# Softmax attention with pooled keys, two expert layers: order of the opening on VectorE and ScalarE

## The chip, the cores and the metric

One Trainium2 chip, one NeuronCore of it. The metric is device microseconds of one execution of the whole program, lower is better. TensorE (PE) multiplies, VectorE (DVE), ScalarE (ACT) and GpSimd (POOL) do elementwise work, SyncE (SP) issues all DMAs.

## The reference

Three stages, each on the output of the one before. All inputs are float32 but the weights, which are float64 and are converted on the chip.

```python
# 1. attention, q/k/v (8, 8, 576, 64): keys and values are means over 8 neighbours
k_p = k.reshape(B, H, Sp, 8, D).mean(axis=3)          # Sp = 72
v_p = v.reshape(B, H, Sp, 8, D).mean(axis=3)
attn = softmax(q @ k_p.T / sqrt(64));  x = attn @ v_p  # x: (4608, 512) after regrouping
# 2. expert layer: w_in (512, 2048), w_out (2048, 512)
g = relu(x @ w_in) ** 2;  y = g @ w_out
# 3. soft mixture: phi (512, 32), w1 (8, 512, 1024), w2 (8, 1024, 512)
logits = y @ phi;  d = softmax over tokens;  c = softmax over slots
slot_out = relu((d.T @ y) @ w1[e]) @ w2[e];  out = c @ slot_out
```

## The kernel before, in words

The 4608 tokens are 36 tiles of 128. Per tile, attention is six steps (`att_qT`, `att_sc`, `att_exp`, `att_norm`, `att_aT`, `att_av`): TensorE turns q (line 188), multiplies it with the pooled keys `kb` (line 204); VectorE takes the maxima `mx` (line 211), ScalarE the exponentials `es`, eight of 72 columns (line 215); VectorE normalises (lines 236 to 238); TensorE turns the weights (line 269), ScalarE copies them to `aT` (line 270), TensorE multiplies with the pooled values `vp` (line 281). The result x goes to SBUF as a rounded high part `xh`, cast by ScalarE (line 288), and a low part `xl`, subtracted by VectorE (line 289).

The first layer is cut into units (t, j): tile t times chunk j of w_in, one of 4 chunks of 512 columns. A unit is 12 matmuls (line 400) over 4 rows kk of the chunk with x and w each in a high and a low part, into one of two PSUM banks `l`. Behind it ScalarE takes the relu `r` (line 412), and the square `g` is made either on VectorE, from the bank and `r` (line 419), or on ScalarE from `r` alone (line 421); the table on the line that sets `sq` chooses. The order of the units is written out in `units`: (0, 0), (0, 1), (1, 0), (3, 1), (3, 0), (1, 1), (2, 0), (0, 2), ..., and from tile 4 on two tiles at a time.

Ahead of its first unit a chunk is converted from float64, one row (0, kk), (1, kk), ... after the other (`conv_in`, `to_f32`): a first step on ScalarE (line 306), two mask steps (lines 307 and 310), a product (line 314), an add (line 317) and a last step (line 318) on VectorE, where table `AE` sends some adds to GpSimd ("P"). Then ScalarE casts the high part (line 349) and GpSimd subtracts the low part (line 350). GpSimd's reads and writes here are of SBUF only, as are those of lines 307 to 318.

The keys and values of the first batch are pooled at the start: keys by TensorE (line 138); values half by TensorE (`pool_v`, line 154, copied out by ScalarE in line 155) and half by VectorE (`pool_v_dve`, line 161). All loads are issued by SyncE in program order: k, q of tile 0, chunk 0, v, q of tile 1, chunk 1. Chunk 2 and 3 follow when their staging buffers `st` are free. In the opening the order of the steps of tiles 0 to 3 comes from `seq`, sorted by places, with the conversions of chunks 0 and 1 at the places in `CP`. The framework then orders the instructions of each engine by a timeline of its own, within data dependencies; `tc.high_priority` and `tc.issue_after` shift that order. Later steps hang at numbered slots of the units (`at`), and the conversions of chunks 2 and 3 follow a relu (`paced`).

Of the kernel before, what the change touches and what calls it, by code (L numbers as in the profile page):

```python
# [17 lines left out]
def kernel(  # L18
# [21 lines left out]
    P = 128  # L40
# [17 lines left out]
    AE = "VVPVVPVPPVVVVPVV"  # L58
    CP = ((5, 6, 6, 6), (19, 19, 22, 23))
# [124 lines left out]
    def att_qT(t):  # L184
# [46 lines left out]
    def att_norm(t):  # L231
# [26 lines left out]
    def att_aT(t):  # L258
# [7 lines left out]
        for half in range(2):  # L266
# [3 lines left out]
            nc.scalar.copy(  # L270
# [30 lines left out]
    def to_f32(src, dst=None, eng=None):  # L301
        hi, lo = src[:, :, 1], src[:, :, 0]
# [19 lines left out]
        return dst  # L322
# [67 lines left out]
    def l1_half(t, j, half):  # L390
# [8 lines left out]
        for i in range(half * n, (half + 1) * n):  # L399
            nc.tensor.matmul(hp_t[t, j], steps[i][0], steps[i][1], start=(i == 0), stop=(i == 2 * n - 1))  # L400
        if half == 1:
# [8 lines left out]
            sq = "VVVAVAVV"[2 * j + t % 2]  # L410
# [424 lines left out]
    kb_from(0, pk0)  # L835
# [189 lines left out]
```

## Time and profile before

| | us |
|---|---|
| median of 3 runs | 817.59 |
| lowest, highest | 813.96, 825.13 |
| profiled execution, its own time | 814.64 |
| its span in the profile | 812.9 |
| TensorE busy | 759.5 (93%) |
| VectorE busy | 518.0 (64%) |
| ScalarE busy | 394.2 (48%) |
| GpSimd busy | 161.8 (20%) |

The profiled execution's own time holds some 1.7 us around the span. Busy shares are means over the whole program; the opening and the rest are far apart, which the rows below show by stretch. PEclk is the granted clock of TensorE as a share of 2.4 GHz.

### The profile page before, as it was taken

How to read it: one execution, taken by the hardware profiler on the slowest of the kernel's cores; microseconds unless marked ns; L12 is line 12 of the kernel's file. 1: busy time of each engine (PE TensorE's matmuls, PEld its weight loads, DVE VectorE, ACT ScalarE, POOL GpSimd, SP SyncE). 2: the span in 40 equal slices, each digit the busy share in tenths (PEclk: the TensorE clock that was granted, in tenths of full speed). 3: DMA queues.
4: the chain of work that ended last, by engine and by line, in shares of the span. 5: the costliest groups of instructions: out<-in, count | busy, mean ns of one | idle time of the engine just before them, and what ended most of it. 6: DMA issues, size and time to landing. Idle time of an engine off the chain costs nothing. (4 is left out here: it accounts for less than half of the span.)

```text
span 812.9 us, 14793 instructions
## 1 busy us (share of the span) xinstructions
PE 759.5 (93%) x5352; PEld 525.5 (65%) x5352; DVE 518.0 (64%) x1033; ACT 394.2 (48%) x1143; POOL 161.8 (20%) x172
## 2 busy tenths in 40 slices
PE   6699999979999999998999999979999999998993
PEld 6477677757667776675666766746666766663552
DVE  5986865586626777685858687685676564424333
ACT  3664555335547473454546462762565643331232
POOL 2532512067513300035005402400000000000000
PEclk8689999999999999999999999989999999999996
DMA  9755734657635884887597797757438424969999
GB/s 278 248 173 193 221 129 148 228 165 250 206 120 158 228 234 130 260 224 178 175 290 227 193 273 203 193 187 213 131 124 278 144 91 158 352 250 321 372 360 313
DMA packets 180857, 175.12 MB, mean 215 GB/s; under 512 B 47152, under 2 KB 138288, under 8 KB 180784
## 3 DMA queue, kind: packets, MB, share of 16 engines
q1 hardware_dynamic: 180784, 174.17, 68.6%
q8 instruction: 43, 0.70, 0.4%
q14 instruction: 30, 0.25, 0.1%
HBM read 126.94 MB, written 47.19 MB: 214 GB/s over the span
## 5 line engine op out<-in xcount | busy, mean ns | idle before, releaser
L400 PE MATMUL l<-w,xh 128*128 128x512 f32 x1152 | 383.7, 412 | 7.1 <-DVE g L419 6.0
L400 PEld LDWEIGHTS l<-w,xh 128*128 128x128 f32 x1152 | 208.3, 190 | 79.6 <-issue 21.4
L400 PE MATMUL l<-w,xl 128*128 128x512 f32 x576 | 229.0, 398 | 0.0
L412 ACT ACTIVATE r<-l 128x512 f32<-128x512 f32 x144 | 86.5, 601 | 167.9 <-PE l L400 165.7
L400 PEld LDWEIGHTS l<-w,xl 128*128 128x128 f32 x576 | 108.8, 189 | 26.0 <-issue 1.0
L254 ACT COPY aT<-turned 32x256 f32<-32x256 f32 (+1 forms) x168 | 67.8, 403 | 22.2 <-DVE turned L263 20.0
L419 DVE TENSOR_TENSOR g<-l,r 128x512 f32<-128x512 f32 x75 | 51.1, 684 | 42.3 <-ACT r L412 35.9
L131 POOL TENSOR_TENSOR kv<-kv 72x512 f32<-72x512 f32 x40 | 52.8, 1323 | 96.3 <-DMA kv<-in_v_dram 65.8
L456 DVE STREAM_TRANSPOSE turned<-turned 128x1024 f32<-128x1024 f32 x39 | 47.8, 1231 | 6.3 <-DMA turned<-g_dram 6.3
L215 ACT ACTIVATE es<-att,mx 128x72 f32<-128x72 f32 x120 | 36.9, 335 | 21.0 <-DVE mx L211 20.9
L317 POOL TENSOR_TENSOR tmp<-tmp 128x512 f32<-128x512 f32 x21 | 28.6, 1362 | 80.4 <-DVE tmp L314 80.4
L215 ACT ACTIVATE es<-gT,mx 128x72 f32<-128x72 f32 x120 | 36.8, 327 | 10.9 <-DVE mx L211 10.7
L419 DVE TENSOR_TENSOR tmp<-l,r 128x512 f32<-128x512 f32 x33 | 22.6, 685 | 28.2 <-ACT r L412 16.7
L256 DVE COPY aT<-turned 32x256 f32<-32x256 f32 (+1 forms) x120 | 35.9, 299 | 4.6 <-PE gT L281 2.9
L350 POOL TENSOR_TENSOR w<-tmp,w 128x512 fp32r<-128x512 f32 x16 | 29.0, 1822 | 45.6 <-ACT w L349 41.3
L133 POOL TENSOR_TENSOR kp<-kv 72x128 f32<-72x128 f32 x20 | 10.1, 523 | 130.5 <-PE att L174 130.5
L456 DVE STREAM_TRANSPOSE tmp<-tmp 128x1024 f32<-128x1024 f32 x25 | 30.7, 1230 | 4.1 <-DMA tmp<-g_dram 4.1
L132 POOL TENSOR_TENSOR kv<-kv 72x256 f32<-72x256 f32 x40 | 31.3, 791 | 0.7
L552 PE MATMUL misc<-g,d 128*32 128x512 f32 x134 | 25.8, 631 | 6.0 <-DVE d L542 5.9
L238 DVE TENSOR_TENSOR es<-es,rs 128x576 f32<-128x576 f32 x36 | 30.5, 846 | 1.0
L307 DVE TENSOR_SCALAR tmp<-tmp 128x512 uint32<-128x512 uint32 x32 | 17.6, 549 | 18.8 <-ACT tmp L306 18.8
L204 PE MATMUL gT<-kb,qT 128*128 128x144 f32 (+1 forms) x176 | 27.3, 306 | 0.0
(188 smaller groups left out, 1138.4 us busy)
## 6 DMA issues: line engine op xcount, KB each, us to landing
g_dram<-g SPq DMA_DIRECT2D x95, 256.0 KB
turned<-g_dram SPq DMA_DIRECT2D x156, 128.0 KB
w<-in_moe_w_dram SPq DMA_DIRECT2D x32, 512.0 KB
tmp<-g_dram SPq DMA_DIRECT2D x100, 128.0 KB
w<-in_moe_w_dram SPq DMA_DIRECT2D x6, 2048.0 KB
g_back<-g_dram SPq DMA_DIRECT2D x10, 1024.0 KB
kv<-in_k_dram SPq DMA_DIRECT2D x32, 288.0 KB
kv<-in_v_dram SPq DMA_DIRECT2D x32, 288.0 KB
```

The source lines that it names most:

```text
L131: eng.tensor_tensor(out=x[:, :, 0:4], in0=x[:, :, 0:4], in1=x[:, :, 4:8], op=ALU.add)
L132: eng.tensor_tensor(out=x[:, :, 0:2], in0=x[:, :, 0:2], in1=x[:, :, 2:4], op=ALU.add)
L215: nc.scalar.activation(out=es[:, e], in_=sv[:, h], func=AF.Exp, bias=mx[:, e:e + 1], accum_out=rsum[:, t % 8, e, 0:1],)
L238: nc.vector.tensor_tensor(out=es, in0=es, in1=rs.unsqueeze(2).to_broadcast([P, H, SP]), op=ALU.mult)
L254: nc.scalar.copy(out=dst, in_=src)
L256: eng[e].tensor_copy(dst, src)
L317: (eng or nc.gpsimd).tensor_tensor(out=mag, in0=mag, in1=low, op=ALU.add)
L350: nc.gpsimd.tensor_tensor(out=w[:, 1, kk], in0=c, in1=w[:, 0, kk].bitcast(F32), op=ALU.subtract)
L400: nc.tensor.matmul(hp_t[t, j], steps[i][0], steps[i][1], start=(i == 0), stop=(i == 2 * n - 1))
L412: nc.scalar.activation(out=r, in_=hp, func=AF.Relu, scale=1.0 / (R * R if sq == "V" else R))
L419: mark["sq"] = nc.vector.tensor_tensor(out=dst, in0=pre, in1=src, op=ALU.mult)
L456: nc.vector.transpose(out=gc.rearrange("p (n i) -> p n i", i=32), in_=gc.rearrange("p (n f) -> p n f", f=32))
```

## The change

It does five things, all in the first 170 us. The conversion is cut into four parts that can be placed singly (`f32_steps`, `conv_steps`). A new function `opening` writes the order out: tile 0's keys, scores, exponentials and normalisation get high priority, the pooling of v and the parts of chunk 0's conversion are placed behind marks of tile 0's attention, unit (0, 0) comes ahead of tile 1's scores, and chunk 1's conversion stands around tile 3's attention in the text. Row 2 of chunk 0 has its add on VectorE, not on GpSimd (`AE`). Rows 2 and 3 of chunk 0 are loaded behind v. All squares of tiles 0 to 5 are on ScalarE, where before 6 of 24 were.

```diff
-    AE = "VVPVVPVPPVVVVPVV"
+    AE = "VVVVVPVPPVVVVPVV"
...
     def to_f32(src, dst=None, eng=None):
+        steps = f32_steps(src, dst, eng)
+        for _ in range(3):
+            dst = next(steps)
+        return dst
+
+    def f32_steps(src, dst=None, eng=None):
...
         nc.scalar.activation(out=val, in_=hi.bitcast(F32), func=AF.Copy, scale=2.0 ** -112)
+        yield
...
+        yield
         (eng or nc.gpsimd).tensor_tensor(out=mag, in0=mag, in1=low, op=ALU.add)
...
-        return dst
+        yield dst
...
+    def conv_steps(j, kk):
...
+        steps = f32_steps(st_t["in", j][:, kk], eng=eng[AE[4 * j + kk]])
+        for _ in range(3):
+            c = next(steps)
+            yield
         nc.scalar.copy(out=w[:, 0, kk], in_=c)
         nc.gpsimd.tensor_tensor(out=w[:, 1, kk], in0=c, in1=w[:, 0, kk].bitcast(F32), op=ALU.subtract)
+        yield
...
-            sq = "VVVAVAVV"[2 * j + t % 2]
+            sq = "A" if t < 6 else "VVVAVAVV"[2 * j + t % 2]
...
-    load_w("in", 0)
+    load_w("in", 0, 0, 2)
     for i in range(NPAIR):
         load_kv(v, raw_v, 0, i)
+    load_w("in", 0, 2, 4)
...
-    kb_from(0, pk0)
...
-    seq = [(p, 1, lambda kk=kk, j=j: conv_in(j, kk)) for j in range(PC) for kk, p in enumerate(CP[j])]
-    seq += [(1, 0, v0)]
-    seq += [(i, 2, lambda i=i: steps[i % 6](i // 6)) for i in range(24)]
...
+    def opening():
+        conv = {(j, kk): conv_steps(j, kk) for j in range(PC) for kk in range(KD)}
+
+        def go(j, kk, n=4):
+            for _ in range(n):
+                next(conv[j, kk])
...
+        early(kb_from, 0, pk0)
+        go(0, 0, 2)
+        early(att_qT, 0)
+        go(0, 0, 1)
+        behind([("qT", 0), "kbA"], go, 0, 0, 1)
+        early(att_sc, 0)
+        go(0, 1, 1)
+        behind(["kbV"], go, 0, 1, 2)
+        behind([("es", 0)], go, 0, 1, 1)
+        early(att_norm, 0)
+        for i in range(0, NPAIR, 2):
+            behind([("sc", 0), ("es", 0)], pool_v, 0, i, kvp)
+            behind([("mx", 0) if i == 0 else ("norm", 0)], pool_v_dve, 0, i + 1, kvp)
+        go(0, 2, 1)
+        behind([("mx", 0)], go, 0, 2, 2)
+        behind([("es", 0)], go, 0, 2, 1)
+        early(att_aT, 0)
+        early(att_av, 0)
+        go(0, 3, 3)
+        behind([("aT", 0)], go, 0, 3, 1)
+        for half in range(2):
+            l1_half(0, 0, half)
+        att_qT(1)
+        behind([("aT", 0)], att_sc, 1)
+        att_norm(1)
+        behind([("l1", 0, 0)], att_aT, 1)
+        att_av(1)
+        for t in (2, 3):
+            att_qT(t)
+            for kk in range(2):
+                if t == 3:
+                    go(1, kk)
+            att_sc(t)
+            att_exp(t)
+            att_norm(t)
+            att_aT(t)
+            for kk in range(2, 4):
+                if t == 3:
+                    go(1, kk)
+            att_av(t)
+
+    opening()
```

The line numbers of the changed kernel differ by 1 to 15 in the lines named here; its orders below have its own numbers. VectorE in the program before, from the copy of tile 0's keys to its first maxima (`kb_119` are the keys, `vp` pooled values, `mx` maxima, `tmp` steps of the conversion):

```order
L167 COPY kb_119<-att 64x4x72
L318 SCALAR_TENSOR_TENSOR tmp<-tmp 128x512
L161 TENSOR_REDUCE vp<-kv_150 72x128
L314 SCALAR_TENSOR_TENSOR tmp<-st,tmp 128x512
L307 TENSOR_SCALAR tmp<-tmp 128x512
L310 TENSOR_SCALAR tmp<-tmp 128x512
L161 TENSOR_REDUCE vp<-kv_150 72x128
L211 TENSOR_REDUCE mx<-gT 128x4 x2
L314 SCALAR_TENSOR_TENSOR tmp<-st,tmp 128x512
```

VectorE in the changed program, the same stretch:

```order
L166 COPY kb_119<-att 64x4x72
L313 TENSOR_SCALAR tmp<-tmp 128x512
L316 TENSOR_SCALAR tmp<-tmp 128x512
L320 SCALAR_TENSOR_TENSOR tmp<-st,tmp 128x512
L324 TENSOR_TENSOR tmp<-tmp 128x512
L210 TENSOR_REDUCE mx<-gT 128x4
L325 SCALAR_TENSOR_TENSOR tmp<-tmp 128x512
L210 TENSOR_REDUCE mx<-gT 128x4
L160 TENSOR_REDUCE vp<-kv_148 72x128
L313 TENSOR_SCALAR tmp<-tmp 128x512
L316 TENSOR_SCALAR tmp<-tmp 128x512
L313 TENSOR_SCALAR tmp<-tmp 128x512
```

The maxima stand ahead of both reductions of v now (the second one is further down), where before they stood behind them, and the steps of rows 2 and 3 of chunk 0 come after the maxima.

ScalarE in the program before, from the first conversion steps to tile 0's exponentials (`es_121`; the first step of a row reads the loaded `st`, the cast writes `w_297`, chunk 0):

```order
L306 ACTIVATE tmp<-st 128x512 x3
L349 CAST w_297<-tmp 128x512
L192 ACTIVATE qT<-gT 128x512
L168 COPY kb_119<-att 64x4x72
L306 ACTIVATE tmp<-st 128x512
L349 CAST w_297<-tmp 128x512
L155 COPY vp<-misc 72x128 x2
L192 ACTIVATE qT<-att 128x512
L306 ACTIVATE tmp<-st 128x512
L215 ACTIVATE es_121,rsum<-gT,mx 128x72 x8
L349 CAST w_297<-tmp 128x512
```

ScalarE in the changed program, the same stretch (`w_245` is chunk 0 there):

```order
L311 ACTIVATE tmp<-st 128x512
L191 ACTIVATE qT<-gT 128x512
L311 ACTIVATE tmp<-st 128x512
L167 COPY kb_119<-att 64x4x72
L363 CAST w_245<-tmp 128x512
L311 ACTIVATE tmp<-st 128x512 x2
L214 ACTIVATE es_121,rsum<-gT,mx 128x72 x8
L363 CAST w_245<-tmp 128x512
L154 COPY vp<-misc 72x128
L191 ACTIVATE qT<-att 128x512
L311 ACTIVATE tmp<-st 128x512
```

The exponentials are ahead of both copies of `vp` and of the cast of row 1, and behind the first steps of all four rows of chunk 0.

ScalarE in the program before, from tile 3's copies of `aT` to its x and two units behind (`l_570` is unit (0, 1), `l_602` (1, 0), `l_631` (3, 1), `l_657` (3, 0), `w_577` chunk 2):

```order
L270 COPY aT<-att 72x512 x2
L192 ACTIVATE qT<-gT 128x512
L349 CAST w_577<-tmp 128x512
L288 CAST xh<-att 128x512
L146 COPY kb_120<-att 64x72
L412 ACTIVATE r<-l_631 128x512
L306 ACTIVATE tmp<-st 128x512
L421 ACTIVATE g<-r 128x512
L412 ACTIVATE r<-l_657 128x512
```

ScalarE in the changed program, the same stretch:

```order
L269 COPY aT<-att 72x512 x2
L427 ACTIVATE r<-l_570 128x512
L427 ACTIVATE r<-l_602 128x512
L311 ACTIVATE tmp<-st 128x512
L436 ACTIVATE g<-r 128x512
L287 CAST xh<-att 128x512
L436 ACTIVATE g<-r 128x512
L145 COPY kb_120<-att 64x72
L363 CAST w_577<-tmp 128x512
L427 ACTIVATE r<-l_631 128x512
L311 ACTIVATE tmp<-st 128x512
L436 ACTIVATE g<-r 128x512
```

Two relus, a first conversion step and a square stand between tile 3's copies and its cast now, and each relu is followed by a square of its own.

## Rows read from the trace of the kernel before

**Rows 1.** Table of stretches: from:to us, length, busy us of engines (instructions), PEclk, DMA share, GB/s
```profile
core 0: us, PE busy (x) PEld busy (x) DVE busy (x) ACT busy (x) POOL busy (x), PEclk, DMA share, GB/s
10.00:20.00 10.00, 5.44 (x39) 5.12 (x34) 9.04 (x15) 4.98 (x9) 3.08 (x2) 0.77 1.03 324
...
30.00:40.00 10.00, 6.97 (x36) 4.76 (x36) 9.97 (x17) 5.57 (x14) 4.69 (x4) 0.50 0.71 234
40.00:50.00 10.00, 9.90 (x47) 8.04 (x48) 7.80 (x11) 5.58 (x11) 4.77 (x4) 0.69 0.78 248
...
60.00:70.00 10.00, 10.00 (x97) 8.06 (x94) 6.55 (x10) 4.80 (x10) 1.28 (x1) 1.00 0.32 85
...
90.00:100.00 10.00, 8.22 (x40) 6.41 (x39) 9.37 (x18) 7.22 (x28) 5.58 (x3) 1.00 0.88 266
```

**Rows 2.** The same table, one stretch from the first conversion to tile 3's weights
```profile
10.90:56.20 45.30, 32.59 (x169) 26.86 (x168) 42.18 (x72) 25.87 (x82) 19.54 (x12) 0.74 0.78 247
```

**Rows 3.** Timeline, TensorE: start us, length us, instruction [idle before <-what ended it]
```profile
15.54 3.69 PE L154 MATMUL misc<-kv,ident 72*72 72x128 f32 x16 [4.56 <-DMA kv<-in_v_dram]
...
31.07 1.89 PE L269 MATMUL gT<-ident,es 128*72 128x128 f32 x8 [5.14 <-ACT w L349]
...
40.10 2.08 PE L400 MATMUL l<-w,xh 128*128 128x512 f32 x4 [1.00 <-ACT xh L288]
...
62.34 0.76 PEld L400 LDWEIGHTS l<-w,xh 128*128 128x128 f32 x4 [0.26 <-ACT xh L288]
```

**Rows 4.** Groups of VectorE, 10.9 to 56.2 us: count | busy us, mean ns | idle before
```profile
L318 DVE SCALAR_TENSOR_TENSOR tmp<-tmp 128x512 uint32<-128x512 uint32 x9 | 9.0, 997 | 0.8 <-POOL tmp L317 0.8
...
L310 DVE TENSOR_SCALAR tmp<-tmp 128x512 uint32<-128x512 uint32 x9 | 5.9, 655 | 0.0
...
L317 DVE TENSOR_TENSOR tmp<-tmp 128x512 f32<-128x512 f32 x5 | 4.4, 872 | 0.0
...
L419 DVE TENSOR_TENSOR g<-l,r 128x512 f32<-128x512 f32 x3 | 2.1, 690 | 0.5 <-ACT r L412 0.5
```

**Rows 5.** Timeline, VectorE and GpSimd: undisturbed steps, a disturbed one, tile 3's weights
```profile
11.27 0.42 DVE L310 TENSOR_SCALAR tmp<-tmp 128x512 uint32<-128x512 uint32 x1
...
13.00 0.68 DVE L317 TENSOR_TENSOR tmp<-tmp 128x512 f32<-128x512 f32 x1
...
14.21 0.68 DVE L318 SCALAR_TENSOR_TENSOR tmp<-tmp 128x512 uint32<-128x512 uint32 x1
...
31.13 2.95 POOL L350 TENSOR_TENSOR w<-tmp,w 128x512 fp32r<-128x512 f32 x2 [1.42 <-ACT w L349]
...
32.87 1.49 DVE L310 TENSOR_SCALAR tmp<-tmp 128x512 uint32<-128x512 uint32 x1
...
55.39 0.76 DVE L238 TENSOR_TENSOR es<-es,rs 128x576 f32<-128x576 f32 x1
```

**Rows 6.** Timeline, ScalarE: a row's first step; first and last of tile 0's exponentials
```profile
11.48 0.67 ACT L306 ACTIVATE tmp<-st 128x512 f32<-128x512 f32 x1 [0.58 <-DMA st<-in_moe_w_in_dram]
...
25.09 0.30 ACT L215 ACTIVATE es<-gT,mx 128x72 f32<-128x72 f32 x1
...
27.37 0.24 ACT L215 ACTIVATION_READ_ACCUMULATOR es<-gT,mx 128x1 f32 x1
```

**Rows 7.** Timeline, two stalls of TensorE and what stood ahead of them
```profile
93.42 0.67 DVE L419 TENSOR_TENSOR g<-l,r 128x512 f32<-128x512 f32 x1
...
94.15 0.73 PE L400 MATMUL l<-w,xh 128*128 128x512 f32 x2 [1.78 <-DVE g L419]
...
170.56 0.21 ACT L146 COPY kb<-att 64x72 f32<-64x72 f32 x1 [4.45 <-DVE kb L145]
...
172.18 1.02 PE L400 MATMUL l<-w,xh 128*128 128x512 f32 x2 [3.85 <-DVE g L419]
```

**Rows 8.** Groups of ScalarE, 10 to 160 us, columns as in rows 4
```profile
L412 ACT ACTIVATE r<-l 128x512 f32<-128x512 f32 x25 | 15.0, 601 | 23.1 <-PE l L400 23.0
...
L270 ACT COPY aT<-gT 72x512 f32<-72x512 f32 x8 | 4.4, 578 | 1.0 <-PE gT L269 1.0
...
L421 ACT ACTIVATE g<-r 128x512 f32<-128x512 f32 x6 | 3.8, 637 | 0.1
```

More of the change, by code (lines that the diff above doesn't have):

```diff
@@ L57 @@
     PEP = (0, 1, 2)
-    AE = "VVPVVPVPPVVVVPVV"
-    CP = ((5, 6, 6, 6), (19, 19, 22, 23))
+    AE = "VVVVVPVPPVVVVPVV"
     CS = ((2, 5, 7, 9), (13, 14, 15, 17))
@@ L166, in kb_from @@
         src = pk[:, :NPAIR * SP].rearrange("p (i s) -> p i s", s=SP)
-        nc.vector.tensor_copy(kb[b % 2][:D, :, 0], src[:D])
-        nc.scalar.copy(out=kb[b % 2][D:, :, 1], in_=src[D:])
+        mark["kbV"] = nc.vector.tensor_copy(kb[b % 2][:D, :, 0], src[:D])
+        mark["kbA"] = nc.scalar.copy(out=kb[b % 2][D:, :, 1], in_=src[D:])
     def make_kb(b):
@@ L203, in att_sc @@
                 for off, n, b, s in parts(t):
-                    nc.tensor.matmul(
+                    mark["sc", t] = nc.tensor.matmul(
                         sc[off:off + n, i * 2 * SP:(i + 1) * 2 * SP],
@@ L214, in att_sc @@
                     e = half * HH + h
-                    nc.scalar.activation(
+                    mark["es", t] = nc.scalar.activation(
                         out=es[:, e], in_=sv[:, h], func=AF.Exp, bias=mx[:, e:e + 1],
@@ L269, in att_aT @@
                 nc.tensor.transpose(pa[:SP, i * P:(i + 1) * P], es[:, half * HH + i], ident)
-            nc.scalar.copy(
+            mark["aT", t] = nc.scalar.copy(
                 out=aT[:, half * HH:(half + 1) * HH].rearrange("p h t -> p (h t)"), in_=pa[:SP]
@@ L344, in conv_in @@
     def conv_in(j, kk):
+        for _ in conv_steps(j, kk):
+            pass
+    def conv_steps(j, kk):
         if kk == 0:
@@ L399, in l1_half @@
         for i in range(half * n, (half + 1) * n):
-            nc.tensor.matmul(hp_t[t, j], steps[i][0], steps[i][1], start=(i == 0), stop=(i == 2 * n - 1))
+            mark["l1", t, j] = nc.tensor.matmul(hp_t[t, j], steps[i][0], steps[i][1], start=(i == 0), stop=(i == 2 * n - 1))
         if half == 1:
@@ L850, in warm_up @@
             nc.tensor.matmul(warm, ident, ident)
-    seq += [(8, 3, warm_up)]
-    for _, _, fn in sorted(seq, key=lambda e: e[:2]):
-        fn()
+        early(kb_from, 0, pk0)
[39 more added lines that the diff above has]
+    opening()
     nc.sync.dma_start(out=phi_sb, in_=phi.rearrange("(k p) s -> p k s", p=P))
@@ L859 @@
         for half in range(2):
-            l1_half(t, j, half)
+            if u:
+                l1_half(t, j, half)
             run_slot(2 * u + half)
```

12 lines of the change are left out of this document (3 added, 9 removed).

## The prediction, written before the run

> **What bounds the kernel now.** I read three views, in this order. The table of stretches [rows 1] shows two regimes. From about 60 us on TensorE is the bound: it is busy 10.00 of 10 us in the stretch from 60 and at granted clock 1.00. Before that it isn't: from 30 to 40 it works 6.97 us at 0.50, the lower of its two levels (1.2 GHz), from 40 to 50 it averages 0.69, and in both stretches it does attention and the first units in pieces, between waits. The engine that is full there is VectorE (9.97 of 10 us). One row for the whole opening [rows 2] says the same: between 10.9 and 56.2 us VectorE is busy 42.18 of 45.30 us, so only 3.1 us of it are idle.
>
> TensorE's own timeline [rows 3] shows what it waits for: 5.14 us ahead of tile 0's turned attention weights at 31.07, the first layer-1 matmul only at 40.10, and, after that, units in pieces until the unit (3, 1) starts at 62.34, released by tile 3's x. That start is my mark. Both programs have done the same TensorE work when it starts (tiles 0 to 3, the units (0, 0), (0, 1) and (1, 0)), and behind it TensorE runs without gaps for 30 us. So the opening is worth as much as that start moves, and what releases it is VectorE's path to tile 3's normalised weights, which end at 56.15 [rows 5], then 6.2 us of transposes, copies and one cast.
>
> **The change, part by part.** *The order on VectorE.* The work up to tile 3's normalisation is counted from the two orders. By then VectorE issues two squares fewer (2 x 0.69 = 1.38 us) and one last conversion step fewer (0.68, it stands later now), and one add more, since row 2 of chunk 0 moves from GpSimd (0.68, undisturbed) [rows 4]: 1.4 us less. With before's 42.1 us of work to 56.15 this leaves 40.7 us. If nothing waited, tile 3's weights would end at 10.9 + 40.7 = 51.6; with as many idle microseconds as now (3.1), at 54.7.
>
> *Which waits go, which come.* The wait for tile 0's weights goes, since scores, maxima and exponentials of tile 0 now stand ahead of chunk 1's conversion. What is late next is the DMA: rows 2 and 3 of chunk 0 are loaded behind v, and on ScalarE their first conversion steps stand ahead of tile 0's exponentials. Row 1 of chunk 0 is there at 11.48 [rows 6]; v (4 x 288 KB) and two rows (2 x 512 KB) are 2.23 MB, at the 324 GB/s of that stretch [rows 1] 6.9 us, so the last row lands near 18.4, its step ends near 19.1, and the eight exponentials (25.09 to 27.6 now, 2.5 us) [rows 6] end near 21.6, 6 us earlier than now. VectorE has 18 instructions ahead of the row sums of these; at 42.18 us over 72 [rows 2] they take 10.5 us from 10.9 on, so it idles about 0.2 us there, or some more if they are disturbed less. A second short wait I expect at tile 1's exponentials, which stand behind tile 0's x on ScalarE. Bounds for its idle time: 0 and 3.1 us; I take 1.5, the middle, as the reorder removes some waits and adds these two. Tile 3's weights then end at 53.1, 3.0 us earlier. If the rows landed only at 24.4, tile 0's exponentials would be no earlier than now.
>
> *What VectorE loses to GpSimd.* Three kinds of steps are far longer in this stretch than undisturbed: the last conversion step takes 997 ns in the mean against 680, the second mask step 655 against 420, the add 872 against 680 [rows 4, 5]. That is 9 x 0.317 + 9 x 0.235 + 5 x 0.192 = 5.9 us of the 42.2. Single rows show why: the mask step at 32.87 takes 1.49 us and ends just after two GpSimd subtractions (31.13 to 34.08) [rows 5]. The change keeps all eight subtractions of chunks 0 and 1 and drops one GpSimd add. Bounds: all 5.9 us gone, or twice as much lost; I keep it as it is, as the same kinds of steps meet in the same stretch. The Trainium skill, GPSIMD Engine Reference, section 8 (Key points), says that GpSimd shares its SBUF interfaces with VectorE and contends with instructions that have two SBUF inputs or use two ports; the trace agrees (997 against 680 ns). By it the same subtractions packed into a shorter stretch would lose no less: my sum stands, and only the end without contention is made less likely.
>
> *From tile 3's weights to the mark.* Now 6.2 us. In the new order TensorE makes tile 2's x and the transposes of tile 4's q ahead of tile 3's weights, no longer behind them. In their place two relus, a first conversion step and a square stand ahead of tile 3's cast on ScalarE. From the end of the weights: transposes 1.0 (8 of them took 1.89 at half clock [rows 3]), two copies 2 x 0.58, two relus 2 x 0.60, the step 0.67, the square 0.64 [rows 6, 8], the cast 0.6: 5.3 us, with 0.1 us for the hand-overs 5.4, so 0.8 us are won. Bounds: 1.8 us lost (relus and square come on top of the 6.2) and 1.8 us won. The unit (3, 1) would start at 62.34 - 3.0 - 0.8 = 58.5.
>
> *Squares on ScalarE.* 18 squares of tiles 0 to 5 leave VectorE (18 x 0.69 = 12.4 us) and cost ScalarE 18 x 0.637 = 11.5 us [rows 4, 8]. Between 60 and 100 ScalarE is busy 4.80 to 7.22 of 10 us [rows 1], which is the cover; without it each 0.64 us is TensorE's. What they bring: a square on VectorE reads the PSUM bank, which is free only after it; on ScalarE the square reads the relu's result, and the bank is free after the relu. One stall in TensorE's stretch is of that kind: 1.78 us at 94.15, ended by the square at 93.42 [rows 7]. It goes: 1.8 us.
>
> *At no cost.* The pooling of v on TensorE moves behind tile 0's scores, into time in which TensorE waits anyway; the warm-up matmuls stand where they stood on TensorE; chunks 2 and 3 are loaded with the same bytes ahead of them. Should TensorE be needed there, one such pooling costs 3.69 us at the lower clock [rows 3], which it costs now as well.
>
> **The sum.** 3.0 + 0.8 + 1.8 = 5.6 us. The profiled execution took 814.64 us for a span of 812.9, so it would take 809.0. The median of the three runs, 817.59, lies 2.95 above it; the same gain from there gives 812.0. I take 810.5, between the two.
>
> **Rivals.** *A, slower: ScalarE becomes the bound of the units.* Its place is the 24 units of tiles 0 to 5, from 60 to about 170 us. Relu and square are 1.24 us per unit on a queue that also waits in order for maxima and key copies. The trace has the mechanism once: ScalarE waits 4.45 us for a key copy at 170.56, the relus behind it are late, and TensorE stands 3.85 us at 172.18 [rows 7]. If the squares push ScalarE into such stalls, each costs 3.85; the second one eats the gain (7.7 against 5.6), and with three it is 11.6 - 5.6 = 6 us slower: 822. For it: 11.5 us more on ScalarE. Against it: it is not full in any stretch shown, and the VectorE steps it waits for come sooner.
>
> *B, no gain: the opening still ends on VectorE.* If idle time is 3.1 again, contention costs 1.5 us more and the 6.2 us stay, the mark doesn't move; if in addition relus wait at 94 as squares do now, nothing is left: 816, the sum's base of 810.5 + 5.6. For it: VectorE is busy 93% of the opening, and most of that is work which stays. Against it: the counted 1.4 us and the square at 93.42.
>
> *C, much faster.* If the conversion steps no longer meet GpSimd's (5.9 us) and VectorE idles 0.5 us, the mark moves 1.4 + 2.6 + 5.9 + 0.8 = 10.7 us; with 1.8 behind it 12.5 us are won: 803.5. The clock would help on that way: now TensorE works at 0.50 from the gap of 5.14 us on, through the whole next stretch [rows 1, 3]. The Trainium skill, TensorE: Matmul & The Clock Gate, section HAM oscillation, says that gaps of waiting put the array back to its lower clock, each time anew. The trace agrees (0.50 from 30 to 40 us). By it a shorter gap is worth more than its length where TensorE is waited for, which would speak for this rival.
>
> *Whether the change does what it says* is to be seen in the orders below the diff: the steps do stand as described, so this gets no chance of its own. But behind 100 us the order on all engines differs in many small places, and TensorE's stalls there (3.85 us at 172.18 the longest that I show) can come or go: 4 us either way, in the range.
>
> **How the numbers follow.** Forecast (3 to 10 us won) 0.58, B 0.22, A 0.10, C 0.10. The forecast's own range is 804 to 816. With A and C, those 4 us, and the spread of the three runs (814 to 825), I take 801 to 822. Over 2% is 16.4 us, about what a measurement of this kernel can tell from no change: faster than 801.2 only the far end of C, 0.06; slower than 833.9 only six stalls of kind A, 0.03; the rest, 0.91, is within it.
>
> **What would show it.** Right: the unit (3, 1) starts between 56 and 60 us, tile 0's exponentials end near 21.6, VectorE is busy 95% of its opening, the conversion steps keep means near 997 and 655 ns, and TensorE has no stall near 90 us that a square ended. Wrong: exponentials after 25 us (then the DMA sets the opening), the unit (3, 1) after 61 us (B), waits of layer 1 on relus of tiles 0 to 5 (A), or a start before 54 us (C).

## The result, and the profile after

The changed kernel takes 808.55 us in the median of 4 runs (808.43 to 812.64), the kernel before 818.34 in 4 (813.96 to 825.13). The ratio, worked out from all runs, is 0.9896, 95% interval [0.9862, 0.9931] (the two medians alone give 0.988): about 1% faster, where 810.5 was forecast. The profiled execution took 808.63 us for a span of 806.0, against 814.64 and 812.9. So the time came out well, but the two terms of the opening behind it did not, and more than half of the gain between these two executions stands behind 349 us, where no edit is.

The table of stretches of the changed kernel, columns as in [rows 1]; its first row answers to [rows 2]:

```profile
10.80:55.10 44.30, 34.21 (x256) 27.42 (x252) 41.42 (x70) 26.81 (x83) 15.18 (x11) 0.85 0.75 236
20.00:30.00 10.00, 7.21 (x34) 6.77 (x35) 8.88 (x16) 4.86 (x23) 1.34 (x1) 0.58 0.99 311
30.00:40.00 10.00, 8.65 (x49) 5.83 (x48) 8.51 (x17) 9.08 (x28) 3.82 (x3) 0.91 0.71 238
40.00:50.00 10.00, 8.30 (x54) 6.11 (x52) 10.00 (x19) 6.32 (x18) 5.70 (x4) 1.00 0.18 52
60.00:70.00 10.00, 9.12 (x91) 7.07 (x88) 7.82 (x14) 5.75 (x12) 1.29 (x1) 1.00 0.42 127
90.00:100.00 10.00, 9.73 (x46) 7.42 (x45) 7.12 (x15) 7.97 (x31) 3.18 (x3) 1.00 0.74 255
```

TensorE's clock is at 0.91 from 30 to 40 us where it was at 0.50, and from 90 to 100 TensorE works 9.73 us where it worked 8.22 [rows 1]. But VectorE's path to tile 3's weights (first row) still has 41.42 us of work and 2.9 us of idle time; 40.7 and 1.5 were forecast. The mark, the start of unit (3, 1), in TensorE's timeline, as in [rows 3]:

```profile
61.43 1.19 PE L415 MATMUL l<-w,xh 128*128 128x512 f32 x4 [0.88 <-ACT xh L287]
```

That is 0.9 us earlier than 62.34; 3.8 were forecast. A mark like that can mislead, so I count in another way too: the starts of the 5th, 18th and 65th relu of layer 1 (line 412 of before, 427 of after) cut a profiled execution into four parts. The relus follow the order of the units, which no kernel here changes. Each number below is the difference of two such starts in one profiled execution, the last one that from the 65th to the span's end.

| us | to 5th relu | 5th to 18th | 18th to 65th | 65th to end | span |
|---|---|---|---|---|---|
| before | 68.2 | 54.4 | 226.3 | 463.9 | 812.9 |
| after | 68.7 | 50.9 | 226.9 | 459.5 | 806.0 |
| after, again (e11) | 68.5 | 50.7 | 227.2 | 459.2 | 805.6 |
| e1 squares | 71.0 | 51.6 | 227.3 | 458.1 | 808.0 |
| e2 opening | 68.3 | 59.1 | 227.7 | 464.5 | 819.6 |
| e3 load | 66.5 | 50.4 | 226.7 | 458.9 | 802.5 |
| e4 chunk 2 | 75.7 | 53.6 | 227.2 | 463.3 | 819.7 |
| e5 bank | 72.8 | 53.6 | 227.4 | 458.0 | 811.8 |
| e6 tile 5 | 71.4 | 56.4 | 224.9 | 461.2 | 813.9 |
| e7 sub | 65.7 | 50.7 | 226.7 | 460.7 | 803.8 |
| e12 sub again | 68.3 | 50.7 | 226.6 | 461.7 | 807.3 |
| e8 tile 8 | 69.5 | 51.3 | 229.0 | 467.0 | 816.8 |
| e9 bank, after | 68.5 | 53.9 | 227.7 | 462.9 | 813.1 |
| e10 all banks | 62.9 | 50.7 | 223.1 | 460.8 | 797.6 |

As they stand, the first part gave nothing (+0.4), the part with the moved squares 3.5 us, and the last, behind 349 us, where not a line was edited, 4.4. But the first two parts don't hold the same TensorE work. The changed kernel does 30 matmuls of a later key pooling (62.55 to 63.70 us) between the mark and its 5th relu; in the kernel before they come behind the 5th relu. So the changed kernel takes 7.2 us from the mark to that relu, the kernel before 5.9, and the second part is shorter by about as much. Up to the 18th relu both have done the same work on TensorE, but for a few matmuls, and there the changed kernel is 3.1 us ahead. The table of stretches from the 5th to the 18th relu, before first, then after:

```profile
68.24:122.68 54.44, 51.80 (x358) 39.99 (x359) 41.24 (x72) 29.79 (x91) 18.64 (x10) 1.00 0.61 198
68.66:119.60 50.94, 50.09 (x327) 38.88 (x328) 35.22 (x61) 35.20 (x100) 16.38 (x10) 1.00 0.65 210
```

TensorE is idle there for 0.9 us instead of 2.6. So 1.8 of the 3.1 us were won by waits that went among these units, and 1.3 us are left for the opening, 0.9 of them at the mark. The two executions of the changed kernel agree part by part within 0.3 us; of the kernel before there is one profile.

### The profile page after: what moved, and what is told of

It is laid out like the page before. It is cut to its first block, busy times and chain, and to the rows that moved or that the text cites. A ratio compares the mean times of both kernels' runs of the same rounds, so it can differ in the third digit from the quotient of the medians.

```text
span 806.0 us, 14772 instructions
## 1 busy us (share of the span) xinstructions
PE 752.2 (93%) x5352; PEld 520.8 (65%) x5352; DVE 515.0 (64%) x1016; ACT 403.8 (50%) x1161; POOL 157.4 (20%) x171
## 4 chain that ended last, share of the span: by engine, by line
PE 64%; DVE 13%; DMA 10%; ACT 3%; SPq 3%; POOL 3%; issue 3%; DVEq 0%; ACTq 0%
PE l L415 38%; PE misc L567 3%; PE pl L496 3%; DMA kv<-in_v_dram 2%; PE misc L999 2%; PE gT L280 2%; PE l L967 2%; PE att L280 2%; PE att L203 2%; DMA g_back<-g_dram 1%; PE gT L203 1%; PE att L496 1%; DMA qt<-in_q_dram 1%; DMA turned<-g_dram 1%; DMA st<-in_moe_w_in_dram 1%
## 5 line engine op out<-in xcount | busy, mean ns | idle before, releaser
L434 DVE TENSOR_TENSOR g<-l,r 128x512 f32<-128x512 f32 x57 | 38.8, 685 | 27.2 <-ACT r L427 20.9
L324 POOL TENSOR_TENSOR tmp<-tmp 128x512 f32<-128x512 f32 x20 | 28.5, 1424 | 70.6 <-DVE tmp L320 62.3
L434 DVE TENSOR_TENSOR tmp<-l,r 128x512 f32<-128x512 f32 x33 | 22.7, 687 | 22.8 <-ACT r L427 16.4
L364 POOL TENSOR_TENSOR w<-tmp,w 128x512 fp32r<-128x512 f32 x16 | 24.8, 1556 | 54.1 <-ACT w L363 54.1
L436 ACT ACTIVATE g<-r 128x512 f32<-128x512 f32 x54 | 34.2, 635 | 0.9
L237 DVE TENSOR_TENSOR es<-es,rs 128x576 f32<-128x576 f32 x36 | 32.5, 903 | 0.8
L210 DVE TENSOR_REDUCE mx<-gT 128x4 f32<-128x288 f32 x38 | 16.6, 445 | 22.5 <-PE gT L203 22.2
```

What stands on the lines that cost most here:

```text
L237: mark["norm", t] = nc.vector.tensor_tensor(out=es, in0=es, in1=rs.unsqueeze(2).to_broadcast([P, H, SP]), op=ALU.mult)
L434: mark["sq"] = nc.vector.tensor_tensor(out=dst, in0=pre, in1=src, op=ALU.mult)
L436: nc.scalar.activation(out=dst, in_=src, func=AF.Square)
```

## The experiments

Three groups of four kernels (e1 to e4, e5 to e8, e9 to e12), each group on one chip, each timed beside the kernel before there (medians of before: 817.13, 820.47 and 818.27 us). The first asks which part of the change earned the gain; the later ones ask why, and whether there is more.

**e1: the squares alone.** The kernel before with

```diff
-            sq = "VVVAVAVV"[2 * j + t % 2]
+            sq = "A" if t < 6 else "VVVAVAVV"[2 * j + t % 2]
```

> The kernel before with one edit: all squares of tiles 0 to 5 on ScalarE. Theory S (the gain is made by the squares, between 85 and 110 us, where the changed kernel's trace wins 3 us, and the opening gives nothing): 3 to 5 us faster than before, 813 to 815 against 818, the stall of 1.78 us ended by a square near 94 us gone, the unit (3, 1) still starts near 62. Rival O (the reordered opening makes the gain): within 1 us of before.

812.63 us, ratio 0.9915 [0.988, 0.9951]. The squares alone, in the old opening, make the kernel faster. TensorE is busy 10.00 of 10 us from 90 to 100, and the part from the 5th to the 18th relu, with the same TensorE work, shrinks from 54.4 to 51.6 us. That is not the whole of it: the last part is 5.8 us shorter, and the mark stands at 64.51, not near 62, at a granted clock of 0.78 from 50 to 60 us.

**e2: the opening alone.** The changed kernel with

```diff
-            sq = "A" if t < 6 else "VVVAVAVV"[2 * j + t % 2]
+            sq = "VVVAVAVV"[2 * j + t % 2]
```

> The changed kernel with the old table of squares (6 of 24 on ScalarE, 18 on VectorE). Theory S: within 2 us of before (818), the stall near 94 us is back. Rival O: 5 to 9 us faster than before, the unit (3, 1) at 60 us or earlier. A third reading, that the order of instructions behind 200 us makes a part of it by accident: the sum of this gain and that of the squares alone misses 9 us by 3 us or more, either way.

821.91 us, ratio 1.0046 [1.0018, 1.0074]: slower than before. TensorE's timeline shows where, a stall of the kind in [rows 7], but longer:

```profile
91.61 1.22 PE L415 MATMUL l<-w,xh 128*128 128x512 f32 x2 [4.74 <-DVE g L434]
```

and VectorE's timeline what stood ahead of that square:

```profile
87.45 2.24 DVE L325 SCALAR_TENSOR_TENSOR tmp<-tmp 128x512 uint32<-128x512 uint32 x2
89.61 0.44 DVE L210 TENSOR_REDUCE mx<-gT 128x4 f32<-128x288 f32 x1
90.87 0.69 DVE L434 TENSOR_TENSOR g<-l,r 128x512 f32<-128x512 f32 x1 [0.81 <-ACT r L427]
```

Behind the new opening VectorE meets the squares together with the conversion of a later chunk. The 5th to the 18th relu take 59.1 us instead of 54.4; behind the stall TensorE's granted clock is at 0.50 from 92 to 96 us, which is a part of that. Neither S nor O holds, and the two gains (4.5 us won in e1, 4.8 lost here) miss 9 us by far, as the third reading has it; the stall shows a cause other than accident. So the squares are not a small extra of the change: without them its opening costs time.

**e3: chunk 0 whole ahead of v.** The changed kernel with

```diff
-    load_w("in", 0, 0, 2)
+    load_w("in", 0)
     for i in range(NPAIR):
         load_kv(v, raw_v, 0, i)
-    load_w("in", 0, 2, 4)
```

> The changed kernel with all four rows of chunk 0 loaded ahead of v, as before. The order on the engines stays, but for one first conversion step on ScalarE that moves ahead of the copy of tile 0's keys. In the changed kernel ScalarE waits 3.00 us for row 2 at 18.23 and tile 0's exponentials start at 20.21. Theory V (VectorE's work sets the start of the unit (3, 1), not the loads): exponentials at 17.5 or earlier, the unit (3, 1) moves by less than 1.5 us from 61.4, the time within 1 us of 808.5. Rival D (the loads of rows 2 and 3 hold the opening): the unit (3, 1) 2 to 3 us earlier, the time 2 to 3 us shorter.

808.78 us, ratio 0.9858 [0.981, 0.9907]. In the changed kernel ScalarE's timeline has the wait for rows 2 and 3 ahead of tile 0's exponentials:

```profile
18.23 0.68 ACT L311 ACTIVATE tmp<-st 128x512 f32<-128x512 f32 x1 [3.00 <-DMA st<-in_moe_w_in_dram]
19.52 0.67 ACT L311 ACTIVATE tmp<-st 128x512 f32<-128x512 f32 x1 [0.61 <-DMA st<-in_moe_w_in_dram]
20.21 0.32 ACT L214 ACTIVATE es<-gT,mx 128x72 f32<-128x72 f32 x1
```

In e3 these exponentials start at 17.53, and unit (3, 1) at 59.29, 2.1 us earlier than in the changed kernel, as rival D has it. One profile a side does not settle the size. The kernel e8 (below) has e3's order on all four engines up to this mark, and there the exponentials start at 20.44 and unit (3, 1) at 62.22. The pooling of the first keys shows the difference, e3 first:

```profile
9.40 3.59 PE L137 MATMUL att<-ident,kv 72*64 72x72 f32 x106
```

```profile
9.74 6.74 PE L137 MATMUL att<-ident,kv 72*64 72x72 f32 x106
16.52 0.45 DVE L166 COPY kb<-att 64x288 f32<-64x288 f32 x1 [2.64 <-PE att L137]
```

TensorE's granted clock is 1.00 from 10 to 20 us in e3 and 0.50 in e8, and VectorE's copy of the keys waits for it. In the five kernels here that load chunk 0 whole ahead of v (e3, e7, e8, e10, e12) tile 0's exponentials start between 17.1 and 20.4 us, in the five with the changed kernel's loads (after, e11, e2, e4, e9) between 20.0 and 22.3. So the loads do hold tile 0; that they cost the mark 2 us is not shown, and the ratios of e3 and of the changed kernel have intervals that overlap.

**e4: chunk 2's first row later.** The changed kernel with

```diff
-    CS = ((2, 5, 7, 9), (13, 14, 15, 17))
+    CS = ((4, 5, 7, 9), (13, 14, 15, 17))
```

> The changed kernel with the first row of chunk 2 converted two slots later (4 for 2), behind the next unit's relu. In the changed kernel its cast stands ahead of tile 3's copies on ScalarE and waits 2.31 us for a VectorE step that takes 1.75 us beside a GpSimd subtraction. Theory C (this cast holds tile 3's x): the unit (3, 1) starts 2 to 3 us earlier, near 59, and the time falls 1 to 3 us below 808.5. Rival: VectorE's other work holds it, the start moves by less than 1 us, and chunk 2 comes later for the unit (0, 2), up to 2 us longer.

813.88 us, ratio 0.9948 [0.9915, 0.9982]: no gain over the changed kernel, rather a loss. Its profiled execution took 821.52 us, the longest of its twelve (809.46 the shortest), so it does not speak for the median. In it TensorE's clock falls, and stays low while TensorE is busy:

```profile
50.00:60.00 10.00, 8.56 (x47) 6.08 (x46) 5.25 (x8) 5.24 (x22) 3.35 (x3) 0.75 0.60 211
60.00:70.00 10.00, 10.00 (x89) 7.96 (x89) 5.81 (x10) 4.74 (x10) 1.73 (x1) 0.50 0.37 108
```

The cast did move out of the way (it is done at 54.35), but the copies behind it came no earlier, as TensorE itself, at the lower clock, was late. What the cast costs by itself stays open.

**e5: the bank.** The kernel before, in which VectorE's squares of tiles 0 to 5 read the relu's copy `r` alone:

```diff
-                nc.scalar.activation(out=r, in_=hp, func=AF.Relu, scale=1.0 / (R * R if sq == "V" else R))
+                nc.scalar.activation(out=r, in_=hp, func=AF.Relu, scale=1.0 / (R * R if sq == "V" and t >= 6 else R))
...
-            dst, src, pre = g, r, hp if sq == "V" else r
+            dst, src, pre = g, r, hp if sq == "V" and t >= 6 else r
```

> The kernel before, in which VectorE still makes the squares of tiles 0 to 5 that it made, but out of the relu's copy r alone, so that the matmuls' PSUM bank is free after the relu on ScalarE. Theory bank: what e1 won between 85 and 110 us (about 3 us) came from the bank being handed back without VectorE's queue; the stall of 1.78 us behind g at 94 us goes, TensorE's busy share of 90:100 rises from 8.2 to 9.5 or more, and the time falls to about 814. Rival VectorE: the gain came from VectorE having 18 squares less to do; then units up to 110 us start where those of before do and the time stays at 817 (815 to 819).

814.47 us, ratio 0.9931 [0.9903, 0.9959]. The stall is gone and TensorE works 10.00 us from 90 to 100, as the bank theory has it. But the part from the 5th to the 18th relu is only 0.8 us shorter than before's (TensorE's idle time in it is 1.2 us instead of 2.6); what this kernel gained in its profile stands in the last part (458.0 against 463.9). The median alone would have told a tidier story than the trace.

**e6: a control.** The kernel before, in which the three VectorE squares of tile 5 alone move:

```diff
-            sq = "VVVAVAVV"[2 * j + t % 2]
+            sq = "A" if t == 5 else "VVVAVAVV"[2 * j + t % 2]
```

> The kernel before with the three VectorE squares of tile 5 alone on ScalarE. Up to 110 us it should run as before does (within 1 us). Theory order: the 4 to 5 us that after and e1 won behind 300 us (the 5.2 us stall behind d near 540 and the one near 377) came from a shifted order and not from those squares; then one of the two stalls or both are gone or changed here too, and the time is 811 to 815. Rival squares: the late gain needs all of tiles 0 to 5 relieved; then both stalls are as in before and the time is 816 to 819.

818.33 us, ratio 0.9996 [0.9968, 1.0024]. The stalls are all there (1.79 us behind `g` near 98, 1.39 behind `aT` near 379, 5.17 behind `d` near 542). That it would run as before does up to 110 us was wrong, though: its order is the same as before's on all four engines up to the mark, and yet the mark stands at 65.50, 3.2 us later, with TensorE's granted clock at 0.50 from 20 to 50 us. A small shift of the program's text does not by itself bring the late gain; my order theory as put there fell. It need not be the squares either: e8 moves more of them and has that stall again.

**e7: no GpSimd in the opening.** e3 with

```diff
-    AE = "VVVVVPVPPVVVVPVV"
+    AE = "VVVVVVVVPVVVVPVV"
...
-        nc.gpsimd.tensor_tensor(out=w[:, 1, kk], in0=c, in1=w[:, 0, kk].bitcast(F32), op=ALU.subtract)
+        (nc.vector if j < 2 else nc.gpsimd).tensor_tensor(out=w[:, 1, kk], in0=c, in1=w[:, 0, kk].bitcast(F32), op=ALU.subtract)
```

> e3_load (the changed kernel with chunk 0 whole ahead of v) with GpSimd's sums and low subtractions of chunks 0 and 1 on VectorE. Theory contention: VectorE's steps beside GpSimd lose about 8 us in the opening (0.42 and 0.68 us become 1.5 and 1.7); VectorE takes over 8 subtractions and 2 sums at 0.68, so 6.8 us, but loses none, and the casts no longer wait for a GpSimd step of 1.5 to 3.1 us; unit (3,1) starts at 57 to 58 instead of 59.3 and the time is 1 to 2 us below e3's. Rival load: VectorE is the bound of the opening and the 6.8 us count nearly whole; unit (3,1) starts at 62 or later and the time is 3 us or more above e3's.

803.35 us, ratio 0.9824 [0.9786, 0.9861], with the mark at 58.71; see e12, where the same kernel ran again.

**e8: two more tiles of squares.** e3 with

```diff
-            sq = "A" if t < 6 else "VVVAVAVV"[2 * j + t % 2]
+            sq = "A" if t < 8 else "VVVAVAVV"[2 * j + t % 2]
```

> e3_load with the squares of tiles 6 and 7 on ScalarE as well. Theory: the stalls of 3.0 to 3.8 us behind g near 165 us, which are VectorE squares of tile 6 and later, go as the one at 94 did; TensorE's share of 160:170 rises from 7.0 to 8.5 or more, and the time is 2 to 4 us below e3's (805 to 807). Rival: ScalarE or something else ends last in those units (a stall of the same size under another name), and the time stays at e3's 808.8 within 1 us.

816.55 us, ratio 0.9967 [0.9937, 0.9996]. Neither side holds. In e3 the stall behind `g` near 165 was only 1.51 us, and TensorE's share of 160:170 was 8.49 (the 3.0 and 7.0 in the expectation are the changed kernel's); here the stall shrank to 0.34 us behind `r` and the share rose to 9.65, yet the later parts grew (229.0 and 467.0 us), with stalls that e3 does not have, 5.17 us behind `d` near 544 among them.

**e9: the bank, behind the new opening.** e2 with e5's edit, from the changed kernel

```diff
-            sq = "A" if t < 6 else "VVVAVAVV"[2 * j + t % 2]
+            sq = "VVVAVAVV"[2 * j + t % 2]
...
-            dst, src, pre = g, r, hp if sq == "V" else r
+            dst, src, pre = g, r, hp if sq == "V" and t >= 6 else r
```

with the relu's scale as in e5.

> The changed kernel with the old table of squares, in which VectorE makes those of tiles 0 to 5 out of the relu's copy r alone: e2_opening but for the bank. Theory bank: the stall of 4.74 us behind g at 91.6 us in e2 goes though VectorE has as much to do, TensorE's share of 80:100 rises from 7.2 to 9.3 or more, units at 97 us start within 2 us of those of the changed kernel, and the time is 809 to 814. Rival VectorE: behind the changed opening VectorE itself is late (9.6 to 9.9 us busy of 10 in 70:90 of e2), the stall comes back under the name r or g through the relu's buffer, and the time stays near e2's, 819 to 823.

818.74 us, ratio 0.9989 [0.9962, 1.0016]. The stall of 4.74 us has become

```profile
89.06 0.73 PE L415 MATMUL l<-w,xh 128*128 128x512 f32 x2 [2.78 <-ACT r L427]
```

and the 5th to the 18th relu take 53.9 us: 5.2 less than in e2 (59.1), 3.0 more than in the changed kernel (50.9). In this part freeing the bank is the larger share. Of its 5.2 us 3.2 are TensorE's idle time (7.0 us in e2, 3.8 here) and 2.0 its busy time, as the clock does not fall behind the stall. Taking the squares from VectorE is the rest, all of it idle time (0.9 us in the changed kernel): ScalarE stands 5.21 us at 87.77 for VectorE's last conversion step, and the relu behind it waits too. The whole time speaks less for the bank: 818.74 us is above the theory's 809 to 814 and next to the rival's 819, the stall did come back under the name of `r`, and by ratio e9 lies 0.6% below e2 but 0.9% above the changed kernel. Its profiled execution, 814.86 us, is 3.9 below its own median.

**e10: all banks.** e7 in which every square on VectorE reads `r` alone, the relu's scale being 1/R throughout:

```diff
-            dst, src, pre = g, r, hp if sq == "V" else r
+            dst, src, pre = g, r, r
```

> e7_sub in which every square of VectorE, those of tiles 6 and up too, reads the relu's copy r alone. Theory bank: the waits behind g of 1.3 to 3.0 us near 165 us and near 198 us go, and the time falls by 1 to 3 us below e7_sub's in this call. Rival order: those waits are a small part, and an order that comes out another way behind 300 us moves the time by 3 to 13 us up or down, as in e8_tile8; then the gain up to 300 us is there in the trace, and the median says nothing of it.

803.44 us, ratio 0.9814 [0.9773, 0.9856], 3.2 us below the same kernel without this edit (e12) on the same chip, with intervals that overlap. The wait behind `g` near 165 us (2.75 us in e12) is 1.06 us behind `r` at 160.96; waits of 1.00 to 1.42 us for other things come up between 175 and 195, and the part from the 18th to the 65th relu falls to 223.1 us from 226.6. Its profile leads by more than that, but 5.4 us of it stand ahead of the 5th relu (62.9 against 68.3), where nothing was edited and TensorE's clock was 1.00 from 10 to 20 us instead of 0.87. By its ratio it is the fastest kernel here, level with e7 within the intervals.

**e11 and e12: the changed kernel and e7, unedited, on one chip.**

> The changed kernel itself, beside the others on one chip. If its opening is what the first profile showed, unit (3,1) starts at 61 to 62 us and the median is 806 to 811.

> e7_sub once more, beside the changed kernel on one chip. Theory contention: unit (3,1) at 58 to 59 us, 2 to 3 us ahead of the changed kernel's, and a median 3 to 6 us below it. If its 803.4 was the better of two equal kernels' draws, the two medians lie within 1.5 us.

809.96 us, ratio 0.9899 [0.9862, 0.9936], and 806.59 us, ratio 0.9855 [0.9822, 0.9887]. The changed kernel's result came out the same again. e12's median lies 3.4 us lower; the two intervals overlap, but with the mark at 58.31 against 61.20 the sign is as expected. What VectorE gains can be read in the groups of VectorE, the changed kernel from 10.8 to 55.1 us (columns as in [rows 4]):

```profile
L325 DVE SCALAR_TENSOR_TENSOR tmp<-tmp 128x512 uint32<-128x512 uint32 x9 | 8.3, 917 | 0.1
L320 DVE SCALAR_TENSOR_TENSOR tmp<-st,tmp 128x512 f32<-128x512 uint32 x9 | 7.8, 878 | 0.1
L324 DVE TENSOR_TENSOR tmp<-tmp 128x512 f32<-128x512 f32 x6 | 5.4, 906 | 0.1
L316 DVE TENSOR_SCALAR tmp<-tmp 128x512 uint32<-128x512 uint32 x9 | 4.8, 535 | 0.0
L237 DVE TENSOR_TENSOR es<-es,rs 128x576 f32<-128x576 f32 x4 | 4.6, 1142 | 0.0
L313 DVE TENSOR_SCALAR tmp<-tmp 128x512 uint32<-128x512 uint32 x9 | 4.4, 493 | 7.7 <-ACT tmp L311 7.7
```

and e12 from 10.8 to 52 us:

```profile
L320 DVE SCALAR_TENSOR_TENSOR tmp<-st,tmp 128x512 f32<-128x512 uint32 x9 | 6.2, 688 | 0.1
L325 DVE SCALAR_TENSOR_TENSOR tmp<-tmp 128x512 uint32<-128x512 uint32 x8 | 5.5, 684 | 0.0
L324 DVE TENSOR_TENSOR tmp<-tmp 128x512 f32<-128x512 f32 x8 | 5.3, 679 | 0.0
L364 DVE TENSOR_TENSOR w<-tmp,w 128x512 fp32r<-128x512 f32 x7 | 4.7, 688 | 0.9 <-ACT w L363 0.9
L313 DVE TENSOR_SCALAR tmp<-tmp 128x512 uint32<-128x512 uint32 x9 | 3.7, 415 | 8.9 <-ACT tmp L311 8.9
L316 DVE TENSOR_SCALAR tmp<-tmp 128x512 uint32<-128x512 uint32 x9 | 3.7, 419 | 0.0
```

Without GpSimd every kind of step falls back to its short time. VectorE has taken over seven subtractions (4.7 us) and two sums by then, and still ends tile 3's weights earlier. How much earlier is best read from executions in which TensorE's granted clock went the same way. In the table e3 and e8 have one order up to the mark, and e7, e10 and e12 have another, without GpSimd in it; all five share their loads.

| | PEclk 10 to 20 us | tile 0's exponentials start | tile 3's weights end | mark |
|---|---|---|---|---|
| e3 | 1.00 | 17.5 | 52.9 | 59.3 |
| e10, no GpSimd | 1.00 | 17.1 | 49.5 | 55.9 |
| e8 | 0.50 | 20.4 | 55.8 | 62.2 |
| e7, no GpSimd | 0.50 | 20.2 | 52.3 | 58.7 |
| e12, no GpSimd | 0.87 | 17.1 | 51.9 | 58.3 |
| after | 0.83 | 20.2 | 55.1 | 61.4 |

In the two pairs of like clock (e3 and e10, e8 and e7; from 30 to 70 us it is 1.00 in all four) the mark comes 3.4 and 3.5 us earlier without GpSimd. In e12's profile, whose clock is 0.83 from 30 to 40 us and 0.75 from 60 to 70, only 1.0 us of that is to be seen against e3. The medians do not show it as clearly: by ratio e12 (0.9855) equals e3 (0.9858), and e7 and e10 lie 0.3% to 0.4% below it with intervals that overlap.

## Why the prediction was right, point by point

The total held, but in good part by luck. Of the 6.9 us between the two spans the opening gave 1.3 (0.9 at the mark), where 3.8 were forecast, and the squares 1.8, as forecast; 3.8 came from behind the 18th relu (4.4 won behind 349 us, where nothing was edited, and 0.6 lost before), which the forecast had as an uncertainty of 4 us either way and not as a gain.

**The order on VectorE (-3.0 forecast, -1.1 measured).** The waits went as said: the loads set tile 0's exponentials, which end at 22.7, 1.1 us later than forecast. Two sizes failed. *Idle time:* 2.9 us instead of 1.5. Nearly all of it is two waits: 1.12 us for tile 0's exponentials, where I had 0.2, and 1.42 for the cast of tile 0's x on ScalarE, where I expected a short one a step later. *Contention:* I kept 5.9 us. By the same three kinds of steps it is 4.5 (9 x 0.237 + 9 x 0.115 + 6 x 0.226, against 680, 420 and 680 ns), but it now also hits kinds that were hardly touched before: the normalisations (1142 ns, in before 749) lose 4 x 0.39 and the products (878, in before 700) 9 x 0.18, 3.2 us more. That more than covers the 0.7 us by which the work (41.42) exceeds the forecast (40.7). A row of VectorE and the two of GpSimd beside it show one such meeting, on the last step to tile 3's weights:

```profile
53.67 1.40 DVE L237 TENSOR_TENSOR es<-es,rs 128x576 f32<-128x576 f32 x1
```

```profile
52.80 1.65 POOL L324 TENSOR_TENSOR tmp<-tmp 128x512 f32<-128x512 f32 x1 [2.09 <-DVE tmp L320]
54.41 1.78 POOL L364 TENSOR_TENSOR w<-tmp,w 128x512 fp32r<-128x512 f32 x1
```

So tile 3's weights end at 55.07, 1.1 us earlier than in before [rows 5].

**From tile 3's weights to the mark (5.4 forecast, 6.4 measured).** The relus, the step and the square stand where I counted them. What I left out is ahead of the copies, in ScalarE's timeline:

```profile
56.77 0.62 ACT L363 CAST w<-tmp 128x512 fp32r<-128x512 f32 x1 [2.31 <-DVE tmp L325]
57.30 0.59 ACT L191 ACTIVATE qT<-gT 128x512 f32<-128x512 f32 x1
57.79 1.05 ACT L269 COPY aT<-att 72x512 f32<-72x512 f32 x2
58.73 1.09 ACT L427 ACTIVATE r<-l 128x512 f32<-128x512 f32 x2
59.70 0.69 ACT L311 ACTIVATE tmp<-st 128x512 f32<-128x512 f32 x1
60.26 0.64 ACT L436 ACTIVATE g<-r 128x512 f32<-128x512 f32 x1
60.78 0.60 ACT L287 CAST xh<-att 128x512 fp32r<-128x512 f32 x1
```

A weight cast waits 2.31 us for a last conversion step, which took 1.75 us beside the subtraction on GpSimd at 54.41, and tile 4's q and tile 3's weights are copied behind it. I had read ScalarE's order from the copies on, not from the instruction ahead of them.

**The mark.** "Both programs have done the same TensorE work when it starts" was right: counted kind by kind, 402 matmuls are in the records ahead of it in both. Behind it the order differs. The 30 matmuls of key pooling cost the changed kernel 1.3 us before its 5th relu, and so the 0.9 us won at the mark read as +0.4 there.

**But before's profiled opening was a lucky one.** Its order up to the mark is e6's, and e6's mark is 3.2 us later. The marks of the four kernels with the old opening (before, e1, e5, e6) are at 62.3, 64.5, 66.2 and 65.5 us, 64.6 in the mean; of four with the changed one (after, e11, e2, e9) at 61.4, 61.2, 62.4 and 62.1, 61.8 in the mean, though e2 and e9 have done 51 and 32 matmuls more by then. The late ones of the old opening have a granted clock below 1.00 somewhere between 50 and 70 us (in e1 0.78 and 0.71, in e5 0.87 and 0.62) or at 0.50 from 20 to 50 (e6). The changed opening can be late too: in e4, which moves one conversion, the mark is at 65.4, and with it the mean is 62.5. So the opening is worth some 2 to 3 us to the median and 0.9 at the mark to this pair of profiles. That fits the gap of 9.8 us between the medians against 6.0 between the profiled executions; with four or five executions a side it is likely, not shown.

**Squares on ScalarE (-1.8 forecast, -1.8 measured).** The mechanism was right: the stall of 1.78 us [rows 7] is 0.27 us now and names the relu, in TensorE's timeline:

```profile
94.81 0.73 PE L415 MATMUL l<-w,xh 128*128 128x512 f32 x2 [0.27 <-ACT r L427]
```

The size was right for this pair of profiles: TensorE's idle time from the 5th to the 18th relu fell by 1.8 us, and the other 1.7 us by which that part is shorter is work that moved. What the forecast did not see is that the two parts depend on each other. The squares are worth 2.8 us of this stretch in the old opening (e1), and behind the new one 8.2 (59.1 in e2 to 50.9), as the new opening pushes VectorE's squares into a chunk's conversion. I priced the squares in before's order and the opening as if they stayed free; the experiments split the 8.2 us into 5.2 for the bank, 2.0 of them at the lower clock behind e2's stall, and 3.0 for VectorE's time.

**Behind 100 us (4 us either way, 3.8 won).** From the 18th relu on the changed kernel wins 3.8 us in its profile (+0.6 and -4.4). It lies within what the forecast left open, but nothing in the forecast made it a gain. Part of it can be read in TensorE's timelines at the same work, before first:

```profile
532.49 0.66 PE L188 MATMUL gT<-ident,qt 128*128 128x128 f32 x4
533.42 0.70 PE L507 MATMUL misc<-plsb,s4rep 128*128 128x256 f32 x2 [0.28 <-DVE acc L562]
533.96 1.14 PE L204 MATMUL gT<-kb,qT 128*128 128x144 f32 x8
540.29 1.07 PE L552 MATMUL misc<-g,d 128*32 128x512 f32 x2 [5.18 <-DVE d L542]
```

then the changed kernel:

```profile
527.49 0.59 PE L522 MATMUL misc<-plsb,s4rep 128*128 128x256 f32 x2
529.06 0.65 PE L187 MATMUL gT<-ident,qt 128*128 128x128 f32 x4 [0.98 <-ACT es L214]
531.40 1.25 PE L203 MATMUL gT<-kb,qT 128*128 128x144 f32 x8 [1.68 <-ACT qT L191]
532.88 0.62 PE L567 MATMUL misc<-g,d 128*32 128x512 f32 x2 [0.24 <-DVE d L557]
```

The logits (`misc<-plsb`) start the chain to `d` through VectorE and ScalarE. In before they stand behind the turning of q, and TensorE waits 5.18 us and goes on at half speed (granted clock 0.50 from 540 to 544 us, 1.07 us for a pair of matmuls); in the changed kernel they stand ahead of it, and the waits sum to 2.9 us at full clock. No edit of the change is near. The stall of 5.2 us is in before, e2, e6, e8 and e9 and in none of the others. Which edit tips the framework's order there was not settled: it is neither "any shift" (e6) nor "the squares" (e8).

**The rivals.** B was nearest to the opening as the profile shows it. A did not come: in the changed kernel no wait of TensorE for a relu of tiles 0 to 5 is over 0.3 us from 62 to 120 us. C was half there: the clock came back (0.91 instead of 0.50 from 30 to 40), but VectorE and ScalarE set the end, so it gave TensorE nothing but waits. For the loss beside GpSimd this case has a price: 1142 ns in the changed kernel against 752 in e12 for a normalisation, 906 against 679 for a sum. The Trainium skill's GPSIMD Engine Reference, section 8 (Key points), names VectorE's instructions with two SBUF inputs as ones that contend with GpSimd; the trace agrees for these two.

## What to carry to other kernels

Two parts of a change that use the same engine should be priced together: this opening loses 0.5% without the squares and gains 1% with them. An elementwise step that reads a PSUM bank holds up TensorE through its whole queue; letting it read a copy in SBUF was 5.2 of the 8.2 us that the squares are worth in that stretch behind the new opening, and 0.8 of 2.8 in the old one. Cutting a program at marks compares like with like only if the same work lies between them: 1.3 us seemed to pass from the opening to the squares here because one key pooling had moved. And where the order of the program is made by a scheduler, compare kernels part by part in the trace: a part that no edit touches can move by 4 us or more, as much as the gain in question.

## What was not expected of the hardware

- Handing VectorE more work made it earlier: with seven more subtractions and two more sums of 0.68 us tile 3's weights end 3.4 us before those of e3 in e10, and 3.5 before those of e8 in e7, at like granted clocks. Beside GpSimd's two-input steps VectorE's own take, in the changed kernel against e12, 535 instead of 419 ns, 878 instead of 688, 906 instead of 679 and 1142 instead of 752.
- TensorE's granted clock can stay at 0.50 while the engine is busy without a gap: in e4 it fell between 54 and 56 us, after two microseconds in which TensorE was busy for 0.85, and was at 0.50 in every stretch of 2 us from 56 to 72, with TensorE busy 2.00 of 2 in each.
- The clock differs between executions of the same order. In e3 and e8 it is 1.00 and 0.50 from 10 to 20 us, 106 matmuls take 3.59 and 6.74 us, and the marks lie 2.9 us apart; in before and e6, also of one order, 3.2. Why an execution goes one way or the other stays open.
